# Attention and two expert layers: values read without the rows that chunks share, gate parts side by side

## The chip, the cores and the metric

The kernel runs on one core of a Trainium2 chip. The metric is the device time of one execution in microseconds; several executions are timed and their median is given. The core has five engines with a queue of instructions each: TensorE (PE, with its weight loads as PEld), VectorE (DVE), ScalarE (ACT), GpSimd (POOL) and SyncE (SP, which here only issues DMA transfers). Instructions of one queue start in order; queues wait for each other through semaphores.

## The reference

Three layers follow each other: a chunked attention, a mixture of experts with two experts for each token, and one with a single expert. All is float32.

```python
def _attn_ref(q, k, v, mem_k, mem_v):          # 4 batches, 8 heads, 768 positions, 64 per head
    chunk, left_ctx, right_ctx = (32, 16, 8)
    for c in range(S // chunk):
        k_full = concat(mem_k, k[l_start:r_end])      # 8 memory rows + up to 56 context rows
        v_full = concat(mem_v, v[l_start:r_end])
        scores = scale * q_c @ k_full.T
        a = softmax(scores)                           # sum + 1e-9
        out[c_start:c_end] = a @ v_full

def _moe_ref(x, w_gate, w_noise, noise, w1, w2):      # 3072 tokens of 512, 8 experts of 1024
    noisy = x @ w_gate + log1p(exp(x @ w_noise)) * noise
    top2, top2_w = two largest, softmax over the two
    out[mask] += top2_w * (relu(x[mask] @ w1[e]) @ w2[e])

def _moe2_ref(x, w_gate, w1, w2):
    expert, gate_w = argmax and softmax probability of x @ w_gate
    out[mask] = gate_w * (relu(x[mask] @ w1[e]) @ w2[e])
```

A chunk's 64 rows of values are 16 rows left of it, its own 32, 8 right of it, and 8 of memory. Neighbouring chunks share rows: the last 24 of a chunk's 56 context rows are the first 24 of the next chunk's.

## The kernel before, in words

The 3072 tokens are 24 tiles (`NT`) of 128 tokens; a tile is four chunks of 32 positions of one batch, with all 8 heads. The attention runs as a pipeline over tiles, written out in `build` (lines 1237 to 1284): iteration `t` does `scores(t)`, `flip(t - 1)`, `exp(t)`, `values(t - 2)`, `turn(t - 3)` and `logits(t - 4)`, in this order on every engine. No scheduler moves anything: each engine's queue has the order of the code.

`load` (line 274) reads a tile's queries, keys and values on the SP queue into one of five buffers `x`: the keys `k` as one transfer of 128 partitions (L278), and the queries with the values as two of 64 partitions each (L283). The lower 64 partitions hold the heads of one half, the upper 64 those of the other; the values of both stand in columns of their own, with zeros opposite (`clear`, lines 264 and 265), so that one matmul serves two heads. A chunk's 64 value rows are the 64 partitions of a half, its columns 260 of the 1040 (`VN`): the host lays the rows out chunk by chunk, those that chunks share several times, with a column of ones behind each head for the sum.

`scores` (L296) multiplies queries by keys into PSUM, and DVE takes the maximum (L303) and subtracts it (L305). `exp` (L311) is one ACT instruction of 512 columns. `flip` (L318, L320) transposes the result. `values` (L334) multiplies by the values, issues `load(t + 5)` for the buffer that has come free, and divides: DVE reads the sums (L340, L341), scales (L343) and casts to float16 (L347); POOL subtracts to get the low half of the number (L348), and SP stores both halves (L354). `turn` (L361, L362) transposes them, and `logits` (L373) multiplies the tile by the router's weights.

Every product is made of three float16 products: a number is a high and a low part, and high x high, high x low and low x high are added. `logits` so does 12 pairs of a weight load and a matmul for each tile, three for each of four slices of 512, into 16 columns of PSUM:

```python
for k in range(4):
    for a, w in ((0, 0), (0, 1), (1, 0)):
        nc.tensor.matmul(self.LG[b][:, j, :], y[:, a, k, :], self.wrh[:, w, k, :], ...)
```

`route` (line 377) runs once for each batch of six tiles: it reads these logits from PSUM (L385, L390), chooses two experts for each token and builds the tables by which the expert layers gather.

In the first expert layer (`Moe1`), 17 groups of up to 416 tokens go through `mlp`: matmuls `ph` (L523), ReLU in two parts (L525, L526), matmuls `py` (L534). `finish` (line 630) scales a block of 128 tokens, scatters it, splits it (`rest`, line 653), transposes it, and multiplies it by the second layer's gate weights, again 12 pairs (L666), now into 8 columns. L669 scales these into SBUF, and they are scattered. `Router2` adds them, takes the maximum and, in `prob` (line 767), the exponential. The second expert layer (`Moe2`) follows. Meanwhile the weights come in by `stage` transfers on SP and are split by ACT (L123) and DVE (L124).

Of the kernel before, what the change touches and what calls it, by code (L numbers as in the profile page):

```python
# [6 lines left out]
F32 = mybir.dt.float32  # L7
# [11 lines left out]
TB = S // 128  # L19
# [5 lines left out]
QV = QN + VN  # L25
# [206 lines left out]

def parts(nc, pool, src, n, name):
# [10 lines left out]
class Attention:  # L244


    def __init__(self, tc, g, qkv, ld, wk):
        nc = self.nc = tc.nc
        c = g.c
        self.tc, self.g, self.qkv, self.ld, self.wk = tc, g, qkv, ld, wk  # L250
        self.EE, self.ET, self.XT, self.LG, self.W = {}, {}, {}, {}, {}
        self.X = [ld.tile([128, 2 * QV + KN], F32, name=f"x{u}") for u in range(LK)]
# [9 lines left out]
    def clear(self, u):  # L262
        x = self.X[u]
        self.nc.vector.memset(x[64:128, KN:KN + QV], 0.0)  # L264
        self.nc.gpsimd.memset(x[0:64, KN + QV:], 0.0)
# [8 lines left out]
    def load(self, t, what="kqv"):  # L274

        x, y = self.X[t % LK], self.qkv[t]
        if "k" in what:
            self.nc.sync.dma_start(x[:, 0:KN], y[:, 0:KN])  # L278
        n = QN * ("q" in what) + VN * ("v" in what)
        for u in range(2):  # L280
            p = slice(64 * u, 64 * u + 64)
            o = KN if u == ("q" in what) else KN + QV - n
            self.nc.sync.dma_start(x[p, u * QV + o:u * QV + o + n], y[p, o:o + n])  # L283

    def scores(self, t):
# [4 lines left out]
        k = x[:, 0:KN].rearrange("p (b k) -> p b k", b=4)  # L290
        q = x[:, KN + VN:KN + VN + 2 * QN].rearrange("p (q b c) -> p b c q", b=4, c=4)
# [30 lines left out]
    def values(self, t):  # L322
# [4 lines left out]
        for a in range(2):  # L327
            for u in range(2):
                for ch in range(4):
                    i = KN + (D + 1) * (4 * ch + 2 * a + u)  # L330
                    v = x[:, i:i + D + 1]
                    v = bass.AP(tensor=v.tensor, offset=v.offset, ap=[v.ap[0], [QV + QN, 2], v.ap[1]])
# [31 lines left out]
    def logits(self, t):  # L364
# [3 lines left out]
        if j == 0:  # L368
            self.LG[b] = self.g.psr.tile([128, TB, 16], F32, name="lg")
        n = 0  # L370
        for k in range(4):
            for a, w in ((0, 0), (0, 1), (1, 0)):
                nc.tensor.matmul(self.LG[b][:, j, :], y[:, a, k, :], self.wrh[:, w, k, :],  # L373
                                 start=(n == 0), stop=(n == 11))
                n += 1

    def route(self, b):
# [3 lines left out]
        l = self.LG.pop(b)  # L381
# [161 lines left out]
class Moe1:  # L543
# [86 lines left out]
    def finish(self, p, gate, idx, group=None, lg=None):  # L630
# [22 lines left out]
        def rest(lg):  # L653
# [7 lines left out]
            if lg is None:  # L661
                lg = g.psr.tile([128, TB, 16], F32, name="lg")[:, 0, 0:E]
# [836 lines left out]
```

## Time and profile before

| what | us |
|---|---|
| three timed runs, median | 1055.11 |
| lowest and highest | 1054.06, 1056.59 |
| the profiled execution, its time | 1055.31 |
| its span in the profile | 1053.5 |
| PE busy | 980.5 (93%) |
| DVE busy | 486.7 (46%) |
| POOL busy | 423.3 (40%) |
| ACT busy | 377.6 (36%) |

The span is the part of the execution from the first to the last recorded instruction; 1.8 us lie around it. Busy time of PE counts pipelined matmuls with modelled ends, so 93% doesn't mean that PE is at its peak. The attention lies in the first 150 us, the first expert layer from there to about 760 us, the second behind it. A mean over the whole span mixes these three, so the views that follow are taken by stretch.

### The profile page before, as it was taken

How to read it: one execution, taken by the hardware profiler on the slowest of the kernel's cores; microseconds unless marked ns; L12 is line 12 of the kernel's file. 1: busy time of each engine (PE TensorE's matmuls, PEld its weight loads, DVE VectorE, ACT ScalarE, POOL GpSimd, SP SyncE). 2: the span in 40 equal slices, each digit the busy share in tenths (PEclk: the TensorE clock that was granted, in tenths of full speed). 3: DMA queues.
4: the chain of work that ended last, by engine and by line, in shares of the span. 5: the costliest groups of instructions: out<-in, count | busy, mean ns of one | idle time of the engine just before them, and what ended most of it. 6: DMA issues, size and time to landing. Idle time of an engine off the chain costs nothing.

```text
span 1053.5 us, 19188 instructions
## 1 busy us (share of the span) xinstructions
PE 980.5 (93%) x7599; PEld 585.0 (56%) x7599; DVE 486.7 (46%) x1015; ACT 377.6 (36%) x601; POOL 423.3 (40%) x420
## 2 busy tenths in 40 slices
PE   4899878999989999999999999989988998999998
PEld 3788755656545555454555555554564564555665
DVE  7567686542413432242234223475564355555511
ACT  1344344222323333233333233344313354454421
POOL 2222232334534454634554445434317255343421
PEclk9999979999999999989999999999998999999999
DMA  9999959745746776766687568489337679988640
GB/s 219 272 281 301 279 142 276 173 91 122 173 102 166 156 178 150 165 134 147 161 180 151 136 150 173 104 247 270 82 121 201 180 189 248 275 169 257 143 63 18
DMA packets 190146, 185.55 MB, mean 176 GB/s; under 512 B 151414, under 2 KB 152310, under 8 KB 190048
## 3 DMA queue, kind: packets, MB, share of 16 engines
q1 hardware_dynamic: 167664, 136.03, 56.4%
q0 software_dynamic: 21952, 48.07, 15.0%
q8 instruction: 62, 1.02, 0.4%
q14 instruction: 36, 0.29, 0.1%
q10 hardware_dynamic: 432, 0.15, 0.1%
HBM read 123.07 MB, written 39.53 MB: 154 GB/s over the span
## 4 chain that ended last, share of the span: by engine, by line
PE 45%; issue 12%; POOL 5%; DMA 4%; DVE 3%; ACT 1%; POOLq 0%; DVEq 0%; ACTq 0%; SPq 0%
PE ph L523 22%; PE py L534 20%; PE pr L716 2%; DMA xt<-x 2%; POOL out_dram L1037 1%; POOL x L1018 1%; DMA stage<-in_v_dram 1%; POOL gs L990 1%; PE lg L666 1%; POOL xp L990 1%; DVE w L124 1%; ACT w L123 1%; DMA xp<-Y,tbr 1%; DVE hT L526 0%; DMA xT<-xg 0%
## 5 line engine op out<-in xcount | busy, mean ns | idle before, releaser
L523 PE MATMUL ph<-xT,w 128*128 128x384 f16 (+3 forms) x2688 | 427.2, 318 | 23.3 <-DVE hT L526 10.8
L534 PE MATMUL py<-w,hT 128*128 128x512 f16 x1800 | 394.0, 379 | 0.0
L523 PEld LDWEIGHTS <-w 128*128 128x128 f16 x2688 | 263.1, 99 | 170.3 <-issue 31.3
L534 PEld LDWEIGHTS <-hT 128*128 128x128 f16 x1800 | 175.7, 98 | 207.3 <-issue 0.3
L526 DVE SCALAR_TENSOR_TENSOR hT<-ph,hT 128x384 f16<-128x384 f32 (+3 forms) x224 | 115.6, 521 | 254.8 <-ACT hT L525 218.1
L124 DVE SCALAR_TENSOR_TENSOR w<-stage,w 128x1024 f16<-128x1024 f32 x128 | 169.1, 1325 | 67.4 <-ACT w L123 62.2
L525 ACT ACTIVATE hT<-ph 128x384 f16<-128x384 f32 (+3 forms) x224 | 102.8, 462 | 232.9 <-PE ph L523 203.4
L123 ACT ACTIVATE w<-stage 128x1024 f16<-128x1024 f32 x128 | 133.5, 1049 | 23.9 <-DMA stage<-in_v_dram 18.5
L634 ACT ACTIVATE y<-py,gs 128x512 f32<-128x512 f32 x48 | 33.0, 687 | 190.4 <-PE py L534 134.1
L637 POOL DMA_INDIRECT Y<-y,t3y x43 | 44.4, 1034 | 115.7 <-ACT y L634 102.2
L655 DVE SCALAR_TENSOR_TENSOR x<-y,x 128x512 f16<-128x512 f32 x50 | 34.5, 690 | 119.8 <-ACT x L651 72.7
L637 POOL DMA_INDIRECT L<-l,t3y x43 | 45.0, 1047 | 101.4 <-DVE l L669 99.0
L1037 POOL DMA_INDIRECT out_dram<-y,tbo x22 | 23.7, 1076 | 128.0 <-ACT y L1036 102.5
L348 POOL TENSOR_TENSOR x<-x,x 128x512 f16<-128x512 f32 x24 | 29.4, 1226 | 112.7 <-DVE x L347 100.3
L296 PE MATMUL s<-x 128*64 128x64 f32 x768 | 50.3, 288 | 22.9 <-DVE x L264 10.6
L591 POOL DMA_INDIRECT Y<-ol,late x48 | 55.4, 1155 | 16.4 <-issue 16.4
L296 PEld LDWEIGHTS s<-x 128*64 128x64 f32 x768 | 47.0, 209 | 24.9 <-issue 23.3
L1036 ACT ACTIVATE y<-py,gs 128x512 f32<-128x512 f32 x27 | 18.5, 685 | 86.1 <-PE py L534 53.8
L565 POOL DMA_INDIRECT xg<-X,t3x x43 | 42.2, 981 | 15.1 <-issue 14.6
L565 POOL DMA_INDIRECT gs<-G,t3g x41 | 38.8, 946 | 12.5 <-issue 12.5
L1018 POOL TENSOR_TENSOR x<-xp 128x512 f32<-128x512 f32 x27 | 36.0, 1354 | 16.2 <-DVE xg L1021 9.9
L334 PE MATMUL o<-x,et 128*32 128x130 f32 x768 | 31.6, 307 | 3.8 <-DVE x L343 3.1
(267 smaller groups left out, 634.9 us busy)
## 6 DMA issues: line engine op xcount, KB each, us to landing
stage<-in_w_dram SPq DMA_DIRECT2D x64, 512.0 KB
stage<-in_v_dram SPq DMA_DIRECT2D x64, 512.0 KB
x<-in_qkv_dram SPq DMA_DIRECT2D x46, 388.0 KB
x<-in_qkv_dram SPq DMA_DIRECT2D x24, 368.0 KB
X<-x SPq DMA_DIRECT2D x24, 256.0 KB
xT<-xg SPq DMA_TRANSPOSE x75
xt<-x SPq DMA_TRANSPOSE x52
Y<-ol,late POOLq DMA_INDIRECT x48
```

The costliest lines, as they stand in the source:

```text
L123: nc.scalar.activation(hi, src, AF.Copy, scale=SW)
L124: return lambda v=nc.vector: v.scalar_tensor_tensor(lo, src, SW, hi, op0=OP.mult, op1=OP.subtract)
L296: nc.tensor.matmul(s[o:o + 64, ch // 2, b], q[:, b, ch], k[:, b, 40 * ch:40 * ch + 64], start=True, stop=True)
L523: nc.tensor.matmul(p[:, :n], w1[:, a, k, f, :], xT[:, b, k, :n], start=(i == 0), stop=(i == 11))
L525: nc.scalar.activation(hT[:, 0, f, :n], p[:, :n], AF.Relu)
L526: nc.vector.scalar_tensor_tensor(hT[:, 1, f, :n], p[:, :n], 0.0, hT[:, 0, f, :n], op0=OP.max, op1=OP.subtract)
L534: nc.tensor.matmul(p[:m], hT[:, a, f, o:o + m], w2[:, c, f, :], start=(i == 0), stop=(i == 23))
L565: self.nc.gpsimd.indirect_dma_start(out=out, out_offset=None, in_=src, in_offset=IO(ap=idx, axis=0))
L591: st = nc.gpsimd.indirect_dma_start(out=self.Y, out_offset=IO(ap=idx[:, i:i + 1], axis=0), in_=z, in_offset=None, bounds_check=2 * N - 1, ...
L637: st = nc.gpsimd.indirect_dma_start(out=dst, out_offset=IO(ap=idx, axis=0), in_=src, in_offset=None, bounds_check=2 * N - 1, oob_is_err=False)
L655: nc.vector.scalar_tensor_tensor(w[:, DM:], y, SX2, w[:, :DM], op0=OP.mult, op1=OP.subtract)
L1018: nc.gpsimd.tensor_tensor(s, x[:, :DM], x[:, DM:], op=OP.add)
```

## The change

Four things change.

1. **Loads.** Queries and keys come as one tensor `qk`, values as two: `va` has the 32 rows of each chunk that no other chunk starts with, once, and `vb` the last 24 rows of the tile's fourth chunk and the 8 memory rows, once. `load` issues seven transfers for three: 64 partitions of keys and lower queries (L289), 64 of keys (L290), 64 of upper queries (L291), and for each half 32 of `va` (L295) and 32 of `vb` (L296).
2. **Copies on the chip.** `spread` is new and stands behind `scores(t)` in each iteration. For each half, POOL copies `vb`'s 260 columns to the three other chunks (L303, 32 partitions), and then writes over 24 of these partitions with the next chunk's rows, which stand in the first 24 partitions one chunk further (L305).
3. **Order of the 64 rows.** Since the 24 shared rows now stand ahead of the 8 memory rows, `exp` writes its 64 columns in three pieces (32, 24 and 8) in the new order.
4. **Gates.** `gating` replaces both loops of 12: the high and the low weights stand side by side, so that the high part of the tokens is loaded once and multiplied by both, into 2n columns, and the low part goes onto the second n. `route` adds the two halves with two more DVE instructions; in the second layer L669 becomes a reduction, and its scale moves into the exponential in `prob`.

```diff
-QV = QN + VN
+QK = QN + KN
+VC = VN // 4
+XK, XQ, XU, XV = VN, VN + KN, VN + QK, VN + QK + QN
...
+def gating(nc, out, xT, w, n):
+    for k in range(4):
+        nc.tensor.matmul(out[:, 0:2 * n], xT[:, 0, k, :], w[:, :, k, :], start=(k == 0), stop=False)
+        nc.tensor.matmul(out[:, n:2 * n], xT[:, 1, k, :], w[:, 0, k, :], start=False, stop=(k == 3))
...
     def clear(self, u):
         x = self.X[u]
-        self.nc.vector.memset(x[64:128, KN:KN + QV], 0.0)
-        self.nc.gpsimd.memset(x[0:64, KN + QV:], 0.0)
+        self.nc.vector.memset(x[64:128, 0:VN], 0.0)
+        self.nc.vector.memset(x[64:128, XQ:XU], 0.0)
+        self.nc.gpsimd.memset(x[0:64, XU:], 0.0)
...
-    def load(self, t, what="kqv"):
-        x, y = self.X[t % LK], self.qkv[t]
-        if "k" in what:
-            self.nc.sync.dma_start(x[:, 0:KN], y[:, 0:KN])
-        n = QN * ("q" in what) + VN * ("v" in what)
+    def load(self, t, what="qv"):
+        x, dma = self.X[t % LK], self.nc.sync.dma_start
+        if "q" in what:
+            dma(x[0:64, XK:XU], self.qk[t, 0:64])
+            dma(x[64:128, XK:XQ], self.qk[t, 64:128, 0:KN])
+            dma(x[64:128, XU:XV], self.qk[t, 64:128, KN:])
+        if "v" in what:
+            for u in range(2):
+                p, o = 64 * u, XV * u
+                dma(x[p:p + 32, o:o + VN], self.va[t, 32 * u:32 * u + 32])
+                dma(x[p + 32:p + 64, o + 3 * VC:o + VN], self.vb[t, 32 * u:32 * u + 32])
+
+    def spread(self, t):
+        x = self.X[t % LK]
         for u in range(2):
-            p = slice(64 * u, 64 * u + 64)
-            o = KN if u == ("q" in what) else KN + QV - n
-            self.nc.sync.dma_start(x[p, u * QV + o:u * QV + o + n], y[p, o:o + n])
+            p, o = 64 * u, XV * u
+            self.nc.gpsimd.tensor_copy(x[p + 32:p + 64, o:o + 3 * VC].rearrange("p (c v) -> p c v", c=3),
+                                       x[p + 32:p + 64, None, o + 3 * VC:o + VN].to_broadcast([32, 3, VC]))
+            self.nc.gpsimd.tensor_copy(x[p + 32:p + 56, o:o + 3 * VC], x[p:p + 24, o + VC:o + VN])
...
     def exp(self, t):
-        self.nc.scalar.activation(e, d, AF.Exp, scale=0.125)
+        for i, o, n in ((0, 0, 32), (32, 40, 24), (56, 32, 8)):
+            self.nc.scalar.activation(e[:, :, :, i:i + n], d[:, :, :, o:o + n], AF.Exp, scale=0.125)
...
     def logits(self, t):
-        n = 0
-        for k in range(4):
-            for a, w in ((0, 0), (0, 1), (1, 0)):
-                nc.tensor.matmul(self.LG[b][:, j, :], y[:, a, k, :], self.wrh[:, w, k, :],
-                                 start=(n == 0), stop=(n == 11))
-                n += 1
+        gating(nc, self.LG[b][:, j], y, self.wrh, 16)
...
     def route(self, b):
-        l = self.LG.pop(b)
+        lg = self.LG.pop(b)
+        l = rr.tile([128, TB, 16], F32, name="l16")
+        V.tensor_copy(l, lg[:, :, 16:])
+        V.tensor_tensor(l, l, lg[:, :, :16], op=OP.add)
...
-            i = 0
-            for k in range(4):
-                for a, c in ((0, 0), (0, 1), (1, 0)):
-                    nc.tensor.matmul(lg, t[:, a, k, :], g.wg2[:, c, k, :], start=(i == 0), stop=(i == 11))
-                    i += 1
+            gating(nc, lg, t, g.wg2, E)
             l = g.mo.tile([128, E], F32, name="l", bufs=4)
-            nc.vector.tensor_scalar(l, lg, 1.0 / (SX2 * SG), None, op0=OP.mult)
+            with nc.allow_low_precision("float32"):
+                nc.vector.tensor_reduce(l, lg[:, 0:2 * E].rearrange("p (a e) -> p e a", a=2), axis=AX.X, op=OP.add)
...
-            nc.scalar.activation(l, l, AF.Exp)
+            nc.scalar.activation(l, l, AF.Exp, scale=1.0 / (SX2 * SG))
...
                 if t < NT:
                     at.scores(t)
+                    at.spread(t)
```

The first place is the SP queue in the steady attention, one tile with its store and the transfer that follows. `X_62` is the stored array, `x_88` and so on are the five buffers, and in brackets stands what an instruction waits for; DMAHW0 to DMAHW7 are the semaphores of earlier transfers, which new transfers take in turn. Before:

```order
L278 DMA x_88<-in_qkv_dram 128x736 [waits DMAHW2_49]
L283 DMA x_88<-in_qkv_dram 64x1552 [waits DMAHW3_49,PE_49]
L283 DMA x_88<-in_qkv_dram 64x1552 [waits DMAHW4_49]
L354 DMA X_62<-x_701 128x1024 [waits DMAHW5_49,Pool_49]
L278 DMA x_89<-in_qkv_dram 128x736 [waits DMAHW6_49]
```

And with the change:

```order
L289 DMA x_88<-in_qk_dram 64x1248 [waits DMAHW0_49]
L290 DMA x_88<-in_qk_dram 64x736 [waits DMAHW1_49]
L291 DMA x_88<-in_qk_dram 64x512 [waits DMAHW2_49]
L295 DMA x_88<-in_va_dram 32x1040 [waits DMAHW3_49,PE_49]
L296 DMA x_88<-in_vb_dram 32x260 [waits DMAHW4_49]
L295 DMA x_88<-in_va_dram 32x1040 [waits DMAHW5_49]
L296 DMA x_88<-in_vb_dram 32x260 [waits DMAHW6_49]
L378 DMA X_62<-x_784 128x1024 [waits DMAHW7_49,Pool_49]
L289 DMA x_89<-in_qk_dram 64x1248 [waits DMAHW0_49]
```

Four transfers of a tile have become eight. Each waits for the one eight places ahead: that was the same transfer two tiles back and is now the same transfer of the tile before. The store still waits for POOL.

The second place is the POOL queue at the same time. Before, it holds one subtraction for each tile:

```order
L348 TENSOR_TENSOR x_536<-x,x_536 128x512 [waits DVE_49,DMAHW5_49,PE_49,Pool_49]
L348 TENSOR_TENSOR x_619<-x,x_619 128x512 [waits DVE_49,DMAHW1_49,PE_49,Pool_49]
L348 TENSOR_TENSOR x_701<-x,x_701 128x512 [waits DVE_49,DMAHW5_49,PE_49,Pool_49]
L348 TENSOR_TENSOR x_783<-x,x_783 128x512 [waits DVE_49,DMAHW1_49,PE_49,Pool_49]
L348 TENSOR_TENSOR x_865<-x,x_865 128x512 [waits DVE_49,DMAHW5_49,PE_49,Pool_49]
```

With the change, four copies stand between one subtraction and the next:

```order
L372 TENSOR_TENSOR x_696<-x,x_696 128x512 [waits DVE_49,DMAHW7_49,PE_49,Pool_49]
L303 COPY x_90<-x_90 32x780 [waits DMAHW4_49,Pool_49]
L305 COPY x_90<-x_90 24x780 [waits DMAHW3_49,Pool_49]
L303 COPY x_90<-x_90 32x780 [waits DMAHW6_49]
L305 COPY x_90<-x_90 24x780 [waits DMAHW5_49,Pool_49]
L372 TENSOR_TENSOR x_784<-x,x_784 128x512 [waits DVE_49,DMAHW7_49,PE_49,Pool_49]
```

The copies of tile `t` (here in `x_90`) wait for that tile's four value transfers, and the subtraction of tile `t - 2` stands behind them.

## Rows read from the trace of the kernel before

**Rows 1.** Busy time by stretch: us, engines' busy time (x count), PE clock, DMA share, GB/s

```profile
20.00:40.00 20.00, 17.90 (x308) 15.07 (x307) 12.87 (x27) 6.88 (x11) 4.81 (x4) 0.91 1.03 262
30.00:85.00 55.00, 50.77 (x923) 44.64 (x923) 35.30 (x107) 24.02 (x35) 11.64 (x10) 0.94 1.03 278
120.00:140.00 20.00, 17.56 (x340) 15.78 (x340) 13.37 (x56) 8.41 (x14) 5.98 (x6) 1.00 0.77 223
300.00:400.00 100.00, 96.86 (x625) 51.34 (x624) 33.40 (x53) 33.72 (x54) 43.80 (x42) 0.98 0.66 149
```

**Rows 2.** Transfers of 30 to 85 us: issues of one kind, count, KB each

```profile
x<-in_qkv_dram SPq DMA_DIRECT2D x22, 388.0 KB
x<-in_qkv_dram SPq DMA_DIRECT2D x11, 368.0 KB
X<-x SPq DMA_DIRECT2D x10, 256.0 KB
```

**Rows 3.** The SP queue's waits of 0 to 140 us: total, times, longest

```profile
SPq L354 <- POOL x L348: 31.2, 15, 6.1
SPq L283 <- DMA x<-in_qkv_dram: 13.6, 16, 1.4
```

**Rows 4.** PE in order of time in the attention: start, us, line, operation

```profile
91.07 1.09 PE L334 MATMUL o<-x,et 128*32 128x130 f32 x32
...
92.55 0.45 PE L373 MATMUL lg<-wr,xt 128*128 128x16 f16 x12
...
92.93 2.08 PE L296 MATMUL s<-x 128*64 128x64 f32 x32
...
95.52 1.42 PE L334 MATMUL o<-x,et 128*32 128x130 f32 x32
```

**Rows 5.** Busy time by stretch at the start, columns as in the first group

```profile
9.20:11.20 2.00, 0.63 (x12) 0.66 (x13) 1.73 (x2) 0.00 (x0) 0.00 (x0) 1.00 0.99 214
13.20:14.40 1.20, 0.00 (x0) 0.00 (x0) 1.05 (x2) 0.09 (x1) 0.00 (x0) 1.00 1.20 303
14.50:16.40 1.90, 1.90 (x32) 1.88 (x32) 1.35 (x1) 0.45 (x1) 0.00 (x0) 1.00 1.04 225
```

**Rows 6.** The tile x from 0 to 90 us: shortest, median and longest issue, ns

```profile
L283 SPq DMA_DIRECT2D x<-in_qkv_dram x38: 465/472/1320, 1.2 to 89.5; - x38
```

**Rows 7.** Groups by line of 0 to 140 us: busy us, mean ns, idle before

```profile
L348 POOL TENSOR_TENSOR x<-x,x 128x512 f16<-128x512 f32 x21 | 24.4, 1163 | 104.4 <-DVE x L347 95.2 <-DVE s L301 4.8 <-PE s L296 4.4
...
L343 DVE TENSOR_TENSOR x<-o,r 128x512 f32<-128x512 f32 x21 | 14.5, 692 | 2.4 <-DVE r L341 0.5
...
L311 ACT ACTIVATE e<-d 128x512 f32<-128x512 f32 x23 | 14.5, 629 | 20.3 <-DVE d L305 18.5 <-DVE r L340 1.5 <-issue 0.3
...
L265 POOL MEMSET x<- 64x1552 f32 x5 | 6.8, 1453 | 0.0
...
L347 DVE CAST x<-x 128x512 f16<-128x512 f32 x21 | 9.0, 427 | 4.0 <-DMA X<-x 3.5
...
L385 ACT ACTIVATE ex<-lg 128x48 f32<-128x48 f32 x3 | 0.6, 205 | 0.0
```

**Rows 8.** PE in order of time in the first expert layer

```profile
221.35 0.45 PE L666 MATMUL lg<-wg,xt 128*128 128x8 f16 x12
221.66 4.06 PE L523 MATMUL ph<-xT,w 128*128 128x384 f16 x24
```

**Rows 9.** The tile lg: shortest, median and longest, ns; first and last start

```profile
L669 DVE TENSOR_SCALAR l<-lg x50: 151/159/168, 208.4 to 756.5; 128x8 f32<-128x8 f32 x50
```

**Rows 10.** The chain that ended last, shares by line

```profile
by line: PE ph L523 21.7%; PE py L534 19.9%; issue 11.8%; PE pr L716 2.1%; DMA xt<-x 1.5%; POOL out_dram L1037 1.4%; POOL x L1018 1.3%; DMA stage<-in_v_dram 1.3%; POOL gs L990 1.1%; PE lg L666 1.1%; POOL xp L990 1.1%; DVE w L124 0.7%; ACT w
```

**Rows 11.** All engines in order of time at the start

```profile
1.13 0.26 DVE L186 CAST diag<-diag_i 128x128 f32<-128x128 int32 x1
...
1.98 6.17 DVE L186 CAST iota<-iota_i 128x144 f16<-128x144 int32 x1
...
2.60 5.46 POOL L265 MEMSET x<- 64x1552 f32 x4
```

More of the change, by code (lines that the diff above doesn't have):

```diff
@@ L244, with __init__ @@
 class Attention:
-    def __init__(self, tc, g, qkv, ld, wk):
+    def __init__(self, tc, g, qk, va, vb, ld, wk):
         nc = self.nc = tc.nc
         c = g.c
-        self.tc, self.g, self.qkv, self.ld, self.wk = tc, g, qkv, ld, wk
+        self.tc, self.g, self.qk, self.va, self.vb, self.ld, self.wk = tc, g, qk, va, vb, ld, wk
         self.EE, self.ET, self.XT, self.LG, self.W = {}, {}, {}, {}, {}
-        self.X = [ld.tile([128, 2 * QV + KN], F32, name=f"x{u}") for u in range(LK)]
+        self.X = [ld.tile([128, XV + VN], F32, name=f"x{u}") for u in range(LK)]
         self.stores = []
@@ L368, in logits @@
         if j == 0:
-            self.LG[b] = self.g.psr.tile([128, TB, 16], F32, name="lg")
-        n = 0
-        for k in range(4):
-            for a, w in ((0, 0), (0, 1), (1, 0)):
-                nc.tensor.matmul(self.LG[b][:, j, :], y[:, a, k, :], self.wrh[:, w, k, :],
-                                 start=(n == 0), stop=(n == 11))
-                n += 1
+            self.LG[b] = self.g.psr.tile([128, TB, 32], F32, name="lg")
+        gating(nc, self.LG[b][:, j], y, self.wrh, 16)
     def route(self, b):
@@ L661, in rest @@
             if lg is None:
-                lg = g.psr.tile([128, TB, 16], F32, name="lg")[:, 0, 0:E]
-            i = 0
-            for k in range(4):
-                for a, c in ((0, 0), (0, 1), (1, 0)):
-                    nc.tensor.matmul(lg, t[:, a, k, :], g.wg2[:, c, k, :], start=(i == 0), stop=(i == 11))
-                    i += 1
+                lg = g.psr.tile([128, TB, 32], F32, name="lg")[:, 0]
+            gating(nc, lg, t, g.wg2, E)
             l = g.mo.tile([128, E], F32, name="l", bufs=4)
-            nc.vector.tensor_scalar(l, lg, 1.0 / (SX2 * SG), None, op0=OP.mult)
+            with nc.allow_low_precision("float32"):
+                nc.vector.tensor_reduce(l, lg[:, 0:2 * E].rearrange("p (a e) -> p e a", a=2), axis=AX.X, op=OP.add)
             scatter(self.L, l)
@@ L1123, in over1 @@
             nc.sync.dma_start_transpose(out=xT.rearrange("p a k q -> p (a k) q"), in_=xg)
-            for _ in mlp(tc, g, key, [128], xT, lambda b, m, p: m1.finish(p, gs, idx[2], lg=pp[:, 400:408])):
+            for _ in mlp(tc, g, key, [128], xT, lambda b, m, p: m1.finish(p, gs, idx[2], lg=pp[:, 400:416])):
                 pass
@@ L1195, in over2, with build @@
                 pass
-def build(tc, qkv, noise, wr, wg2, w1, w2, v1, v2, out):
+def build(tc, qk, va, vb, noise, wr, wg2, w1, w2, v1, v2, out):
     nc = tc.nc
@@ L1225, in build @@
             ld = ctx.enter_context(tc.tile_pool(name="ld", bufs=1))
-            at = Attention(tc, g, qkv, ld, wk)
+            at = Attention(tc, g, qk, va, vb, ld, wk)
             at.ps = ctx.enter_context(tc.tile_pool(name="psa", bufs=1, space=PSUM))
-            at.load(0, "kq")
+            at.load(0, "q")
             at.load(0, "v")
@@ L1448, in layouts, with values @@
     p = pad(inp["v"])
-    w = np.stack([np.concatenate([p[:, :, 32 * c:32 * c + 32], inp["mem_v"], p[:, :, 32 * c + 32:32 * c + 56]], axis=2)
-                  for c in range(S // 32)], axis=2)
-    w = split(w, (TB, 4, 64, D)).transpose(0, 4, 3, 6, 5, 1, 2, 7)
-    v = np.ones(w.shape[:-1] + (D + 1,), f)
-    v[..., :D] = w
-    v = v.reshape(NT, 128, VN)
-    lower, upper = slice(0, 64), slice(64, 128)
-    qkv = np.concatenate([np.concatenate([k[:, lower], v[:, lower], q[:, lower]], axis=2),
-                          np.concatenate([k[:, upper], q[:, upper], v[:, upper]], axis=2)], axis=1)
+    def values(w, c):
+        w = split(w, (TB, c, 32, D)).transpose(0, 4, 3, 6, 5, 1, 2, 7)
+        v = np.ones(w.shape[:-1] + (D + 1,), f)
+        v[..., :D] = w
+        return v.reshape(NT, 64, c * VC)
+    va = values(p[:, :, :S], 4)
+    vb = values(np.concatenate([x for j in range(TB) for x in (p[:, :, 128 * j + 128:128 * j + 152], inp["mem_v"])],
+                               axis=2), 1)
+    qk = np.concatenate([k, q], axis=2)
     def rows(w):
@@ L1466, in layouts @@
     return {
-        "qkv": qkv,
+        "qk": qk, "va": va, "vb": vb,
         "noise": inp["moe_noise"].reshape(NT, 128, E).transpose(1, 0, 2).reshape(128, NT * E),
```

8 lines of the change are left out of this document (4 added, 4 removed).

## The prediction, made before the change was run

> **What bounds the kernel now.** I read four views in this order: the busy table by stretch, the transfers and the SP queue's waits of the attention, PE in order of time, and the groups by line.
>
> The table [rows 1] splits the run. From 20 to 40 us, as in the whole stretch from 30 to 85, the sixteen DMA engines are at their limit (share 1.03), while PE is busy 18 of 20 us: the attention is paced by its transfers, with PE close behind. From 300 to 400 us PE is busy 96.9 of 100 us and DMA two thirds: the first expert layer is paced by PE. What is saved in loads counts in the first stretch, what is saved in matmuls in the second.
>
> From 30 to 85 us the transfers run at 278 GB/s [rows 1]. One tile is a load of 368 KB, two of 388 KB and a store of 256 KB [rows 2], 1400 KB or 1.434 MB: 5.16 us a tile. The SP queue waits most for the subtraction L348 ahead of the store and then for older transfers [rows 3]. PE does one tile at full clock in the 4.45 us from one block of values (91.07) to the next (95.52), of which the logits take 0.38 (92.55 to 92.93) [rows 4]. Over the stretch PE is busy 50.77 of 55 us [rows 1], 4.76 us a tile with the router's matmuls. So if the loads shrink, PE lets 0.4 to 0.5 us a tile through.
>
> **The loads.** A tile's loads go from 1144 KB (1.171 MB) to 312 + 184 + 128 + 2 x (130 + 32.5) = 949 KB (0.972 MB), 17% fewer bytes. But the 368 KB load covered all 128 partitions; now every load covers 64 or 32. Two stretches of the start in which little but a 64-partition load is under way run at 214 and 225 GB/s, one that is mostly the 128-partition load at 303 [rows 5]. With 220 and 303: before 377 kB / 303 + 795 kB / 220 = 1.24 + 3.61 = 4.85 us, and the 0.31 us missing to 5.16 is what the store adds. After: 972 kB / 220 + 0.31 = 4.73 us, a gain of 0.43 us a tile. Lower end: all halves at 214, 4.85 us, gain 0.31. Upper end: the stretch's own 278 GB/s holds for smaller pieces too, which swap halves more often and may overlap: 1.234 MB / 278 = 4.44 us, gain 0.72. It applies to some 20 tiles; the last ones (120 to 140 us, DMA share 0.77 [rows 1]) are paced by something else. PE stands at about 4.7, and two limits so close don't interlock perfectly, so I book the lower end, 0.3 us a tile: **-6.0 us** (up to 24 x 0.72 = 17.3 were the loads alone the bound).
>
> **The SP queue** issues eight transfers a tile for four. An issue of this kind has a median of 0.47 us [rows 6]: the four added ones cost 1.9 us of SP a tile and all eight 3.8, below 4.7. As the order rows show, a transfer waits for the one eight places ahead of it, so one tile is in flight where there were two. Its 4.4 us of queued data cover an issue; I cost it at nothing. If they don't, one bare issue a tile, 0.47 x 20 = 9 us, eats the gain.
>
> **POOL** gets four copies a tile, each 780 elements long. No row shows a POOL copy. Below: the memset L265, 1453 ns for 1552 elements, 0.94 ns each, so 0.73 us. Above: the subtraction L348, which reads two streams, 1163 ns for 512, 2.27 ns each, so 1.77 us [rows 7]. I take 0.75 us: a copy has one stream in and one out, nearer to the memset. Four copies and L348 make 4 x 0.75 + 1.16 = 4.16 us a tile, under 4.73. They stand in the queue ahead of the subtraction of the tile two back, for which the store on SP and the turn on PE one iteration later wait. A tile's values (333 kB at 220, 1.5 us) land behind its keys, so the copies end some 4.5 us after the keys. The cast L347 that the subtraction needs comes after scores and flip (92.93 to 95.52), values (1 us) and L343 with two short DVE instructions (1 us) [rows 4, 7]: 4.6 us after the keys. The cover holds, barely. I cost POOL at nothing.
>
> The Trainium skill (GPSIMD Engine Reference, Engine selection) says that one-input work on this engine runs at roughly line rate; no row here shows it.
>
> **The exponent** in three pieces: L311 takes 629 ns for 512 columns and L385 205 for 48, so 0.91 ns a column and 0.16 us fixed: 3 x 0.16 + 512 x 0.00091 = 0.95 us, 0.32 more [rows 7]. ACT is busy 24 of 55 us [rows 1], and the flip that reads the result comes an iteration later: hidden, 24 x 0.32 = 7.7 us if not. The memsets keep their size.
>
> **The gates.** Each gating goes from 12 load-and-multiply pairs to 8. In the expert layer 12 pairs move the next matmul by 0.31 us (221.35 to 221.66) [rows 8]; there are 50 such blocks [rows 9], a third less is 50 x 0.10 = 5.2 us. The chain that ended last holds 1.1% of 1053.5 us, 11.6 us, in that line [rows 10]; a third is 3.9 us. Between them **-4.5 us**, nearly all in the stretch that PE paces. The attention's 24 blocks (24 x 0.13 = 3.0 us) hide behind the loads. DVE's read L669 becomes a reduction to the same 8 columns, off the path. The router reads its logits through a copy and an addition, each a little over L669's 159 ns [rows 9], four times; DVE's wait for the logits costs nothing, since its next reduction waits for scores that stand behind them on PE. The last router stands on the path: **+0.5 us**. The scale that moves into the exponential costs nothing.
>
> **Sum.** The profiled execution took 1055.31 us, 0.2 us above the median of the runs shown: 1055.3 - 6.0 - 4.5 + 0.5 = **1045.3 us**.
>
> **Rivals.**
> (a) POOL becomes the bound, slower. A DVE cast took 0.26 us, the next 6.17 us while POOL's memsets ran, and it ended when they did [rows 11]: a DVE instruction can stand still for a whole row of POOL's. If L347 (0.43 us [rows 7]) and POOL exclude each other, POOL's turn of a tile is 4c + 1.16 + 0.43, with c for a copy. It passes 5.16 at c = 0.89, and from c = 0.97 it costs more than the gates' net 4.0 and 2.1 us beyond. In the middle of the bounds, c = 1.25: 6.59 us, (6.59 - 5.16) x 20 = 28.6, so 1055.3 + 28.6 - 4.0 = 1080; at c = 1.77 it is 1121. Against it: the memset's price, and that the cast comes when the copies are mostly over. The Trainium skill (SBUF — State Buffer, two separate sides) calls the port pair that these two engines share an exclusive lock, held for a whole instruction; the 6.17 us agree. Chance 0.20.
> (b) The loads gain nothing: every piece runs at the rate of the half loads and the smaller ones lose the rest at their ends. Only the gates count: 1055.3 - 4.0 = 1051.3. For it speak 214 and 225 against 303 GB/s [rows 5]; against it, that even at 214 throughout the bytes give 0.31 us a tile. The Trainium skill (SBUF — State Buffer, The DMA port swizzle) says that 64 partitions reach half of the memory's ports, and 32 no fewer; by that rule, splitting the 368 KB load undoes most of what the missing rows save. The rows agree on the halves. Chance 0.22.
> (c) The rate holds with the bytes: 17.3 us, 1055.3 - 17.3 - 4.0 = 1034; with PE's limit of 0.5 us on 20 tiles 1041; I put it at 1037. Chance 0.13.
> (d) The gates don't do what they say: 12 x 8 columns before, 4 x 16 + 4 x 8 now, the same 96. Were a pair's price its columns, the 4.5 us are gone: 1049.8. Against it: in the attention 12 pairs of 16 columns cost 0.38 us, not twice the 0.31 of 8 columns [rows 4, 8]. Chance 0.05.
>
> **How the numbers follow.** The forecast has the remaining 0.40. A measurement of this kernel can tell about 0.2%, 2.1 us, from no change. Faster: the forecast but for 0.03 of it, (c), (d) and 0.17 of (b): 0.72. Same: 0.05 of (b) and that 0.03: 0.08. Slower: (a), 0.20. The range goes from just under (c), 1036, over (d) and (b) into the foot of (a) (c = 1.02, 1062), which leaves out under 2 in 10.
>
> **What would show it.** Right: the copies L303 and L305 near 0.75 us; tiles every 4.8 to 4.9 us between 30 and 85 us; the gating blocks of the expert layer moving the next matmul by 0.2 us; PE's first expert matmul some 6 us earlier. Wrong: copies over 0.95 us, or POOL busy from end to end of the attention (a); the DMA share still at its limit with fewer GB/s (b); gaps in the DMA share while SP issues (one tile in flight).

## The result, and the profile after

The changed kernel took **1043.17 us** (median of 8 runs, 1035.05 to 1047.39) against 1055.18 for the kernel before on the same chip (8 runs, 1052.65 to 1065.08): ratio 0.9861, 95% interval 0.9827 to 0.9895, so 11 to 18 us less by the interval. 1045.3 was forecast. The profiled execution is the fastest of the eight, 1035.05 us, so the two profiles differ by 20 us where the medians differ by 12.

The same stretches as in [rows 1], columns as there (the cores' engines, then PE's granted clock, DMA share and GB/s):

```profile
20.00:40.00 20.00, 18.05 (x311) 15.20 (x310) 14.06 (x29) 8.78 (x21) 18.46 (x20) 0.91 0.94 238
30.00:85.00 55.00, 48.54 (x847) 41.84 (x843) 40.68 (x107) 23.47 (x51) 46.83 (x51) 0.95 0.95 247
120.00:140.00 20.00, 12.01 (x221) 10.09 (x220) 16.74 (x61) 7.02 (x18) 13.48 (x16) 0.86 0.57 150
300.00:400.00 100.00, 98.07 (x606) 51.40 (x605) 33.89 (x54) 34.03 (x54) 46.56 (x45) 1.00 0.63 154
```

Two things changed in the steady attention. The DMA engines are no longer full, and they move less in the same time (247 GB/s for 278). And POOL, the fifth engine of the row, went from 11.6 to 46.8 us of 55. From 120 to 140 us PE does only 12.0 us of work instead of 17.6. The groups of 0 to 140 us that answer to [rows 7]:

```profile
L305 POOL COPY x<-x 24x780 f32<-24x780 f32 x45 | 40.2, 893 | 2.8
L303 POOL COPY x<-x 32x780 f32<-32x780 f32 x45 | 39.0, 867 | 7.5 <-DMA xg<-X,t1x 3.0 <-DMA x<-in_vb_dram 1.9
L372 POOL TENSOR_TENSOR x<-x,x 128x512 f16<-128x512 f32 x20 | 23.2, 1160 | 16.0 <-DVE x L371 4.1 <-PE misc L467 3.9 <-DMA x<-in_va_dram 2.5
...
L371 DVE CAST x<-x 128x512 f16<-128x512 f32 x21 | 11.8, 561 | 8.5 <-DMA X<-x 7.9
```

A copy takes 0.88 us. The subtraction is as long as before, and the cast ahead of it takes 561 ns instead of 427.

The stores leave at 32.76 us (tile 1) and 78.04 (tile 10), so tiles follow each other every 5.03 us; before it was 32.40 and 81.46, 5.45 us. But the last values of the attention start later, before:

```profile
148.23 1.96 PE L334 MATMUL o<-x,et 128*32 128x130 f32 x32 [2.12 <-DVE x L343]
```

and after:

```profile
152.41 2.04 PE L358 MATMUL o<-x,et 128*32 128x130 f32 x32 [2.56 <-ACT w L125]
```

So in these two executions what the attention had won is gone at its end. Two of PE's waits of 85 to 150 us have grown, one for POOL and one for DVE (total, times, longest; some of such a wait can be made up later, so they don't add up to a loss). Before:

```profile
PE misc L223 <- DVE two L408: 1.7, 1, 1.7
...
PE xp L361 <- POOL x L348: 0.3, 1, 0.3
```

And with the change:

```profile
PE xp L385 <- POOL x L372: 7.2, 4, 5.8
PE misc L225 <- DVE two L430: 4.4, 1, 4.4
```

The longest wait for POOL, 5.8 us, stands behind one subtraction, that of the 20th tile. Here POOL also issues the transfers that gather rows for the first experts (L587; start, us, line):

```profile
129.84 0.43 DVE L371 CAST x<-x 128x512 f16<-128x512 f32 x1
...
130.34 0.96 POOL L587 DMA_INDIRECT xg<-X,t1x  x1 [0.30 <-issue]
...
134.26 0.83 POOL L303 COPY x<-x 32x780 f32<-32x780 f32 x1 [2.95 <-DMA xg<-X,t1x]
...
137.87 1.15 POOL L372 TENSOR_TENSOR x<-x,x 128x512 f16<-128x512 f32 x1
...
139.08 0.61 PE L385 MATMUL xp<-ident,x 128*128 128x128 f16 x4 [5.78 <-POOL x L372]
```

The cast that the subtraction needs ended at 130.27. But four copies stand ahead of the subtraction in POOL's queue, and the first of them started, by the profile, only when the gather had landed. So the subtraction began 7.6 us after its cast. Before, it followed within 0.3 us, behind the same gather:

```profile
129.92 0.96 POOL L565 DMA_INDIRECT xg<-X,t1x  x1 [0.30 <-issue]
...
132.99 0.43 DVE L347 CAST x<-x 128x512 f16<-128x512 f32 x1
...
133.66 1.16 POOL L348 TENSOR_TENSOR x<-x,x 128x512 f16<-128x512 f32 x1 [2.78 <-DVE x L347]
```

At the wait for `two` it is DVE that is late (DVE in order of time):

```profile
101.03 0.71 DVE L424 CAST eid<-i 128x12 f32<-128x12 uint32 x1
101.77 0.26 DVE L427 TENSOR_TENSOR oh<-iota,eid 128x96 f16<-128x96 f16 x1
102.06 0.69 DVE L430 TENSOR_TENSOR two<-oh 128x48 f16<-128x48 f16 x1
```

and POOL in the same stretch:

```profile
100.88 0.83 POOL L303 COPY x<-x 32x780 f32<-32x780 f32 x1
101.76 0.96 POOL L305 COPY x<-x 24x780 f32<-24x780 f32 x1
```

`eid` has 12 columns and takes 0.71 us: it ends as the first copy ends. `two` has 48 and ends with the second. Before, they were short:

```profile
102.09 0.16 DVE L402 CAST eid<-i 128x12 f32<-128x12 uint32 x1
...
102.58 0.18 DVE L408 TENSOR_TENSOR two<-oh 128x48 f16<-128x48 f16 x1
```

In between `oh`, which started with the second copy, kept its usual 0.26, and that copy took 0.96 instead of 0.83.

The gating in the first expert layer, which answers to [rows 8] (eight rows for a block now):

```profile
221.93 0.17 PE L238 MATMUL lg<-wg,xt 128*128 128x16 f16 x1
...
222.11 0.17 PE L239 MATMUL lg<-wg,xt 128*128 128x8 f16 x1
222.14 4.06 PE L545 MATMUL ph<-xT,w 128*128 128x384 f16 x24
```

A block moves the next matmul by 0.21 us, where it was 0.31.

### The profile page after: what moved, and what is told of

The parts are those of the page before. It is cut to its first block, busy times and chain, and to the rows that moved or that the text cites. A ratio compares the mean times of both kernels' runs of the same rounds, so it can differ in the third digit from the quotient of the medians.

```text
span 1033.3 us, 18951 instructions
## 1 busy us (share of the span) xinstructions
PE 963.3 (93%) x7303; PEld 573.2 (55%) x7303; DVE 505.0 (49%) x1028; ACT 382.3 (37%) x649; POOL 510.2 (49%) x516
## 4 chain that ended last, share of the span: by engine, by line
PE 40%; issue 14%; POOL 6%; DMA 4%; DVE 4%; ACT 1%; another core or an unknown queue 0%; POOLq 0%; DVEq 0%
PE py L556 19%; PE ph L545 19%; POOL x L1037 2%; DMA xp<-Y,ter 2%; POOL out_dram L1056 1%; PE pr L735 1%; POOL gs L1009 1%; POOL xp L1009 1%; DMA stage<-in_v_dram 1%; DVE w L126 1%; ACT w L125 1%; DVE hT L548 1%; DMA xp<-Y,tbr 1%; DMA xt<-x 1%; PE lg L238 0%
## 5 line engine op out<-in xcount | busy, mean ns | idle before, releaser
L545 PE MATMUL ph<-xT,w 128*128 128x384 f16 (+3 forms) x2688 | 421.3, 315 | 19.5 <-DVE hT L548 9.1
L613 POOL DMA_INDIRECT Y<-ol,late x48 | 58.0, 1208 | 16.4 <-issue 16.4
L318 PE MATMUL s<-x 128*64 128x64 f32 x768 | 49.8, 291 | 12.2 <-DVE x L274 7.9
L318 PEld LDWEIGHTS s<-x 128*64 128x64 f32 x768 | 46.3, 209 | 13.7 <-issue 9.7
L587 POOL DMA_INDIRECT xg<-X,t3x x43 | 42.1, 980 | 15.1 <-issue 14.6
L303 POOL COPY x<-x 32x780 f32<-32x780 f32 x48 | 41.6, 866 | 7.7 <-DMA xg<-X,t1x 3.0
L587 POOL DMA_INDIRECT gs<-G,t3g x41 | 38.8, 946 | 12.5 <-issue 12.5
L305 POOL COPY x<-x 24x780 f32<-24x780 f32 x48 | 42.7, 890 | 2.9
```

Of the source, the lines that this page charges most:

```text
L305: self.nc.gpsimd.tensor_copy(x[p + 32:p + 56, o:o + 3 * VC], x[p:p + 24, o + VC:o + VN])
L318: nc.tensor.matmul(s[o:o + 64, ch // 2, b], q[:, b, ch], k[:, b, 40 * ch:40 * ch + 64], start=True, stop=True)
L545: nc.tensor.matmul(p[:, :n], w1[:, a, k, f, :], xT[:, b, k, :n], start=(i == 0), stop=(i == 11))
L587: self.nc.gpsimd.indirect_dma_start(out=out, out_offset=None, in_=src, in_offset=IO(ap=idx, axis=0))
L613: st = nc.gpsimd.indirect_dma_start(out=self.Y, out_offset=IO(ap=idx[:, i:i + 1], axis=0), in_=z, in_offset=None, bounds_check=2 * N - 1, ...
```

## The experiments

The runs were made in three groups, each on one chip with runs of the kernel before beside them (medians 1058.64, 1046.92 and 1058.65 us). In the order in which the quoted texts count them, the first to fourth are gates alone, loads alone, copies of five tiles and half of the copies on ACT; the fifth to eighth issues on ACT, whole keys, sixteen pairs and five transfers; the ninth to twelfth gates in the expert layer, five transfers with all copies on POOL, five transfers with whole keys, and the change again. Times don't compare across groups. Ratios do if all kernels move with the kernel before, and why that one moved by 12 us between groups is not known.

**1. Which half of the change pays.** The hunks of the diff for `gating`, `logits`, `route`, `finish` and `prob` alone, put into the kernel before:

> The kernel before with the gates of the change alone (8 pairs for 12, the router's two more DVE instructions, the reduction and the moved scale); loads, copies and exponent as before. Theory A, the terms of the prediction: the gates are worth 4.0 us net, so 1051 against 1055 before, ratio 0.996. Theory B, from the trace of the changed kernel: since the attention there ends no earlier than before (last values at 152.4 us against 148.2), the gates and what hangs on them in the expert layers carry the whole gain of 12 us, so about 1043, ratio 0.988. By both, the attention's blocks of values stay where they were (within 1 us), and a gating block in the expert layer moves the next matmul by 0.20 us instead of 0.31.

And the changed kernel with the loops of 12 put back:

> The changed kernel with the old gates (12 pairs): loads, copies and the exponent in three pieces alone. Theory A: 6 to 8 us under the kernel before, 1047 to 1049, ratio 0.993. Theory B: what the loads win by 85 us is lost by 150 us, so 1053 to 1056, ratio 0.998 to 1.001.

Measured: gates alone 1048.14 us, ratio 0.9885 (0.9845 to 0.9926); loads alone 1056.66 us, 1.0003 (0.9974 to 1.0032). The loads, the copies and the exponent in pieces together gain nothing that can be told, and the gates make the whole difference. Theory B held for the times, theory A fell. What both expected of the attention failed: with the gates alone its last values came at 154.5 us, 6.3 later than before, where 1 us was allowed. The DMA engines were as full as before and moved 270 GB/s instead of 278, so the 148.2 us of before is one execution and no fixed mark (see the last section).

**2. What the copies cost.** The copies of the first five tiles alone (`LK` is 5):

```diff
-                    at.spread(t)
+                    if t < LK:
+                        at.spread(t)
```

> The changed kernel with the copies of the first five tiles only; later tiles use whatever rows stand in those partitions, so the shared rows of their values are not this tile's. Theory B says that the copies on POOL hold up DVE (small instructions of the router take 0.6 to 0.8 us instead of 0.2) and with it the end of the attention: without them the last values come at 140 to 144 us instead of 152.4, and the time falls by 8 to 12 us from the 1043 of the changed kernel, to 1031 to 1035. Its rival, that the rate of the partial loads paces the tiles and POOL is only beside them: same places within 2 us and 1041 to 1045.

The last values came at 142.85 us, 9.6 us earlier than with all copies. Its whole time (1132 us) can't be compared, since other values send the tokens to other experts. The router's rows on DVE of 85 to 150 us (busy us, mean ns), with the change:

```profile
L436 DVE TENSOR_TENSOR vr<-eid,vr 128x12 f32<-128x12 f32 x2 | 1.5, 766 | 0.0
L430 DVE TENSOR_TENSOR two<-oh 128x48 f16<-128x48 f16 x2 | 1.5, 736 | 0.1
```

and without the later copies:

```profile
L430 DVE TENSOR_TENSOR two<-oh 128x48 f16<-128x48 f16 x2 | 0.4, 183 | 0.1
L436 DVE TENSOR_TENSOR vr<-eid,vr 128x12 f32<-128x12 f32 x2 | 0.3, 172 | 0.0
```

So the copies hold DVE up: it is busy 31.3 of the 35 us from 85 to 120 with them, 25.1 without. And the 20th subtraction follows its cast in 0.24 us again. The starts of POOL's subtractions show where the 9.6 us arise. With and without the later copies, the 9th starts at 64.2 and 64.1 us, the 12th at 83.4 and 80.3, the 19th at 127.5 and 120.2, the 21st at 142.8 and 133.4. Most of it, 7.3 us, is lost by the 19th, while DVE is the fuller for the copies, and some 2 us more between the 19th and the 21st, where the copies stand behind the gather. All ten profiled executions with copies in the late tiles have that gap ahead of the 20th subtraction (5.7 to 8.1 us), and the four without have 0.24. But tiles did not come faster early on: 5.11 us each from tile 1 to 10. What paces them there is something else.

**3. Half of the copies on ACT.**

```diff
+            copy = self.nc.scalar.copy if u else self.nc.gpsimd.tensor_copy
-            self.nc.gpsimd.tensor_copy(...)
+            copy(...)
```

> The changed kernel with the two copies of the upper half on ACT instead of POOL. ACT then has about 2.5 + 2 x 0.87 = 4.2 us of work in a tile, POOL 2 x 0.88 + 1.16 = 2.9 instead of 4.7. Theory B: half of what the copies cost comes back, 4 to 6 us, so 1037 to 1039. The rival, that ACT's own work (exponent, flip, turn) comes late behind copies that wait for DMA: 1043 to 1050, with PE waiting for et or xp of ACT.

1039.75 us, 0.9844 (0.9803 to 0.9886), too near the change's 0.9861 to tell apart by the time; the last values say more: 147.1 us, 5.3 earlier than the change's profile, about half of the 9.6, as theory B had it.

**4. What paces the tiles.** Issues of L291 and L296 moved from SP to ACT (`other` is SP's queue for the first five tiles, then ACT's):

```diff
-            dma(x[64:128, XU:XV], self.qk[t, 64:128, KN:])
+            other(x[64:128, XU:XV], self.qk[t, 64:128, KN:])
...
+                other(x[p + 32:p + 64, o + 3 * VC:o + VN], self.vb[...])
```

> The changed kernel with three of a tile's seven load transfers (the upper queries and both vb) issued by ACT instead of SP; bytes, pieces and copies stay. Between 30 and 85 us the changed kernel moves 247 GB/s with its queue at 93.7%, and SP waits only 7 us of 55: eight issues of 0.4 to 0.6 us a tile fill it. Theory C, that SP's issues and the one tile in flight open the gaps: queue share over 99%, 260 GB/s or more, a tile 0.3 us sooner, last values 3 to 6 us earlier where the router's delays leave it, time 1038 to 1041 on the scale of 1055 before. Rival D, that partial transfers are slower in themselves: share up to 100%, but GB/s stay within 245 to 252 and the time within 2 us of the changed kernel's ratio of 0.986.

Moving the issues made it worse: 1.0027 (1.0000 to 1.0055), 219 GB/s, last values at 168.4 us. SP's own issues then last 27.9 us of 55, but it waits 24.7 us for older transfers and POOL, 11.9 of them for upper queries that ACT now issues. Of the two longest rows the first is of this kind, the second waits for SP's own transfers:

```profile
SPq L296 <- DMA x<-in_qk_dram: 9.3, 2, 5.8
SPq L290 <- DMA x<-in_qk_dram: 5.8, 5, 2.4
```

That run decides nothing between the theories. Then the keys as one transfer:

```diff
+            dma(x[:, XK:XQ], self.qk[t, :, 0:KN])
+            dma(x[0:64, XQ:XU], self.qk[t, 0:64, KN:])
+            dma(x[64:128, XU:XV], self.qk[t, 64:128, KN:])
```

> The changed kernel with the keys as one transfer of 128 partitions and the queries as two of 64 (seven load transfers a tile, as in the change, and the same bytes). Rival D: the rate of 30 to 85 us rises from 247 to 255 GB/s or more at the same share of the queue, time 2 to 4 us less, 1039 to 1041. Theory C: as many issues and as many gaps, 244 to 250 GB/s, time within 2 us of the change, ratio 0.984 to 0.988.

Time and rate stayed (0.9868, 0.9832 to 0.9904; 247 GB/s), as theory C had it, but the DMA engines became idler, which neither theory had said. The hardware queue of 30 to 85 us (packets, MB, share of the 16 engines), in the change and with whole keys:

```profile
q1 hardware_dynamic: 6274, 13.45, 93.7%
```

```profile
q1 hardware_dynamic: 6965, 13.45, 84.3%
```

The same 13.45 MB need a tenth less of the engines when the keys go to 128 partitions, and the tiles come no faster for it: 4.93 us each. The Trainium skill (SBUF — State Buffer, The DMA port swizzle) says that 64 partitions reach half the ports; the two shares agree that halves cost engine time. They also show that engine time was not the limit here.

**5. Fewer transfers.** Values next to queries in memory, so that five transfers carry a tile's loads:

```diff
+            dma(x[64:128, XK:XQ], ku)
+            dma(x[0:32, 0:XU], la)
+            dma(x[32:64, 3 * VC:XU], lb)
+            dma(x[64:96, XU:], ua)
+            dma(x[96:128, XU:XV + VC], ub)
```

> The kernel of the fourth run (upper copies on ACT) with a tile's loads in five transfers instead of seven: own rows with keys and queries of the lower half in one of 32 partitions, the shared rows with theirs in another, the keys of the upper half, and the same two for the upper half, whose chunks stand in reversed order so that vb lies next to the queries. Same bytes. Theory C: SP issues six transfers a tile, about 3 us; queue share over 99% between 30 and 85 us, last values 3 to 5 us earlier than in the fourth run (147.1 us), time 1035 to 1037, ratio 0.981 to 0.983. Rival D: transfers of 32 partitions are no better, 240 to 250 GB/s, ratio 0.984 as in the fourth run, or worse where a load of 300 KB now waits for the values of the tile that leaves the buffer.

1022.14 us, **0.9775** (0.9740 to 0.9809). Queue share 98.4%, 265 GB/s, a tile every 4.78 us, last values at 141.0 us, 6.1 earlier than with seven transfers: more than theory C had promised, as is the ratio (0.9775 for 0.981 to 0.983), with a share a little under its 99%. The same with `copy = self.nc.gpsimd.tensor_copy` for both halves:

> The eighth run's five transfers with all four copies on POOL, as in the change: against the change only the number and the cut of the transfers differ. Theory C: 260 GB/s or more between 30 and 85 us and a tile every 4.7 to 4.8 us there; POOL then has 4 x 0.88 + 1.16 = 4.7 us of it, so it is at its limit too; the router's delays stay, last values at 146 to 149 us, ratio 0.980 to 0.983. Its rival, that the eighth run owes its gain to having half the copies on ACT: 0.985 to 0.988, last values at 151 us and later.

1041.24 us, 0.9828 (0.9784 to 0.9872), but the last values at 152.6 us as in the change: at that place the rival was right, and theory C's 260 GB/s and 4.7 to 4.8 us a tile did not come (243 and 5.20). The first tiles ran at 263 GB/s (20 to 40 us); from 60 to 85 only 207. POOL was as busy there as in the change (19.5 of 25 us), but now SP waited for the subtraction there, ahead of the store, 13.5 us of the 55 from 30 to 85, where in the change it had waited 1.4:

```profile
SPq L389 <- POOL x L383: 13.5, 8, 4.1
```

Fewer transfers help when POOL has room, and not before. And with whole keys besides, ahead of the lower values in the buffer:

```diff
-            dma(x[64:128, XK:XQ], ku)
+            dma(x[:, 0:KN], k)
```

> The eighth run (upper copies on ACT) with the keys again as one transfer of 128 partitions: keys, then for each half own rows with queries and shared rows with queries, five in all, and the same bytes. In the sixth run whole keys took the queue's share from 93.7% to 84.3% at the same 247 GB/s, 293 GB/s at a full queue; so here the transfers alone would need 1.234 MB / 293 = 4.2 us a tile and PE sets the pace with 4.6 to 4.7. Expected: queue share 90 to 95% at 262 to 270 GB/s, last values at 138 to 141 us, ratio 0.974 to 0.978. Rival: PE, DVE and ACT already set the pace in the eighth run, nothing changes, 0.9775.

1027.46 us, **0.9693** (0.9649 to 0.9736): the lowest ratio of all, under the range that was expected, and 20 us below the change in the same group. Queue share 94.8%, 263 GB/s, last values at 139.5 us, 1.5 earlier than with five transfers alone. That whole keys add anything to five transfers is not shown by the time: the two ran in different groups, and the time itself is 5 us longer here than there. The change itself in the same group:

> The changed kernel itself once more, on the chip of these runs: ratio 0.983 to 0.990 as before, last values at 151 to 154 us, 240 to 250 GB/s between 30 and 85 us. What its profile says of PE's clock and of the blocks near 304 and 445 us tells how far the first profile (20 us under that of before, where the medians differ by 12) was a lucky one: if the medians are right, more of its execution is at half clock than there.

1047.29 us, 0.9885 (0.9842 to 0.9927), last values at 154.0 us, 249 GB/s.

The attention of all these kernels in one table. "SP" is the sum of the durations of SP's issues that start from 30 to 85 us, transfers include the store:

| kernel | transfers a tile | copies | queue share, GB/s | SP, us | last values, us | ratio |
|---|---|---|---|---|---|---|
| before | 4 | none | 101.7%, 278 | 21.6 | 148.2 | 1 |
| gates alone | 4 | none | 101.8%, 270 | 18.0 | 154.5 | 0.9885 |
| change | 8 | POOL | 93.7%, 247 | 43.9 | 152.4 | 0.9861 |
| change, again | 8 | POOL | 95.7%, 249 | 46.3 | 154.0 | 0.9885 |
| loads alone | 8 | POOL | 95.2%, 244 | 46.1 | 154.2 | 1.0003 |
| first five copied | 8 | POOL, five tiles | 94.0%, 245 | 47.3 | 142.9 | - |
| half on ACT | 8 | both | 92.7%, 241 | 46.7 | 147.1 | 0.9844 |
| whole keys | 8 | POOL | 84.3%, 247 | 44.7 | 152.3 | 0.9868 |
| five loads | 6 | both | 98.4%, 265 | 31.6 | 141.0 | 0.9775 |
| five loads, POOL | 6 | POOL | 90.1%, 243 | 30.8 | 152.6 | 0.9828 |
| five loads, whole keys | 6 | both | 94.8%, 263 | 31.8 | 139.5 | 0.9693 |

With eight transfers SP issues for 44 to 47 of 55 us, waits only 2 to 7, and the rate stays at 241 to 249 GB/s, whatever the copies or the keys do. With six it issues for 31 to 32 and waits 19 to 21: it is no longer the limit, and where POOL isn't full, 263 to 265 GB/s are moved. Six transfers for eight also let more of a tile be in flight at once. No run separates that from the issues, but with eight SP waits for older transfers 0.8 to 4.7 of 55 us, so the single tile in flight can cost little beside them.

**6. The price of the gates.** Each block of the expert layer twice:

```diff
             gating(nc, lg, t, g.wg2, E)
+            gating(nc, lg[:, 2 * E:], t, g.wg2, E)
```

> The changed kernel with each gating of the expert layer done twice, the second time into columns that nobody reads: 16 pairs for 8 in 50 blocks. By the direct price of a pair (0.0255 us, from 0.204 us for a block of 8) this costs 8 x 0.0255 x 50 = 10 us: 1053, and nothing else changes. Theory E, that blocks of many short instructions also leave PE without instructions behind them where a block stands between the matmuls pr (there the block of before lasts 3.6 and 3.8 us instead of 0.3, and PE runs at half clock after it): 15 to 20 us more than the change, 1058 to 1063, and the blocks near 304, 445 and 590 us last 3.5 us and more.

Sixteen pairs: 1047.45 us, 0.9996 (0.9973 to 1.0019), 0.0128 x 1047 = 13 us more than the whole keys with 8 pairs on the same chip, a little over the direct 10. A block lasts 0.41 us, as the direct price says, and the blocks at the three places are short (0.71, 0.48, 0.49 us): theory E fell in this form. Nor does the time follow the number of pairs alone: 16 pairs cost no more than the 12 old ones of the loads alone (1.0003, in another group), though a block takes 0.41 us with 16 and 0.31 with 12. And the hunks for `gating`, `finish` and `prob` alone, without `logits` and `route`:

> The kernel before with the 8 pairs in the expert layer alone; the router of the attention keeps its 12 pairs and its reads. By the direct price, 50 blocks x 0.10 = 5 us: 0.995. By theory E (some of the time is that PE waits for instructions around three blocks near 304, 445 and 590 us, and runs at half clock behind them) 8 to 12 us: 0.989 to 0.992, with those three blocks together shorter than the 8.4 us of before. The rival that the router's part carries the difference to the 11 us of the first run: 0.995 and the three blocks as before.

1039.70 us, 0.9792 (0.9739 to 0.9844), more than either theory had, and more than the gates with the router's part (0.9885, in another group). So the direct price of 5 us is seen in every trace, and the time moves by more.

Two more terms can be read from PE's rows, in one execution of each kernel: before and loads alone with 12 pairs; gates alone, gates in the expert layer and the change twice with 8. From the start of a block to PE's next other matmul, the blocks of a run sum to 23.2 and 22.4 us with 12 pairs and to 16.4, 13.3, 12.6 and 15.5 with 8, so 7 to 11 us less and not 5. The surplus lies in the three blocks ahead of `pr` matmuls that the expectation names: 8.4 and 7.6 us together with 12 pairs, 6.2, 3.2, 2.5 and 5.4 with 8 (and 1.7 with 16). And the matmuls `ph` and `pr`, the same in number everywhere, are busy 455.2 and 450.9 us with 12 pairs and 448.7, 444.6, 444.5 and 453.4 with 8. The last two are one kernel, so a single execution doesn't tell how much of this the gates cause.

The first profile of the change and the second differ most plainly at the first `pr` matmuls, with the same instructions. First profile:

```profile
301.31 2.77 PE L735 MATMUL pr<-w,rh 128*32 128x512 f16 x24
...
305.94 2.77 PE L735 MATMUL pr<-w,rh 128*32 128x512 f16 x24 [1.58 <-PEq L1079]
```

Second profile:

```profile
303.37 2.77 PE L735 MATMUL pr<-w,rh 128*32 128x512 f16 x24
...
309.57 5.31 PE L735 MATMUL pr<-w,rh 128*32 128x512 f16 x24 [3.15 <-PEq L1079]
```

PE waits there for its own sequencer, 1.58 us or 3.15, and after the longer wait the 24 matmuls take 5.31 us instead of 2.77: the lower of the clock's two levels, 1.2 instead of 2.4 GHz (the granted clock is 0.50 from 309.57 to 314.88 us, and 1.00 in the 2.77 us at 303.37). From the first expert matmul to the end of the last one the two executions of one kernel took 872.0 and 884.5 us. Single executions with 12 pairs took 897 (before) and 888 (loads alone), those with 8 took 868 to 887, and the one with 16 took 883 (the run with copies of five tiles, which sends tokens elsewhere, left out). **What stays open:** why the gates' 5 us become 8 to 16, or 16 to 28 in the expert layer alone. Waits of this kind and the clock behind them are where the traces differ, but no run set them on purpose.

## Why the prediction was right, point by point

The number was right (1045.3 forecast, 1043.17 measured, inside the range), and that was luck: of -6.0 us booked for the loads nothing came, and of -4.0 net for the gates -12.2 did. The two errors, 6.3 and 8.2 us, cancel but for 2.

- **Loads, -6.0 us: failed.** Alone they measured +0.3 us (-2.8 to +3.4). A tile's gain came out inside what was derived, 0.42 us (5.45 to 5.03) for 0.31 to 0.72, but not for its reason: the DMA rate fell from 278 to 247 GB/s and SP set the pace. The old loads, too, took 5.68 and 5.76 us a tile in two other executions (gates alone, gates in the expert layer). What failed is the step "I cost POOL at nothing": the copies cost 9.6 us by the end of the attention, which took the gain back.
- **POOL.** c was 0.88 us, between 0.75 and the 0.97 from which rival (a) wins. 4 x 0.88 + 1.16 = 4.7 us a tile is under the 5.03 that a tile takes, so the turn of a tile never became the bound as (a) priced it. Its mechanism was there all the same, at a place that I hadn't named: the router's many short DVE instructions, each of which can wait out a copy (`two`: 0.74 us for 0.18), and PE behind them. I had looked for the lock only at the cast. "The cover holds, barely" failed as well, at one tile: behind the gather the 20th subtraction started 7.6 us after its cast; elsewhere in that trace it was 2.6 at most. I had not counted the gathers in POOL's queue. The Trainium skill (SBUF — State Buffer, two separate sides) calls the shared ports an exclusive lock; `eid` and `two` ending with the copies agree.
- **SP, "I cost it at nothing": failed.** I reckoned 3.8 us of issues a tile, and they take 43.9 x 5.03 / 55 = 4.0 us: nearly right. What failed is that the transfers in flight would cover them. With 7 of the 55 us of waits and some 4 between issues SP is never ahead. That is why a tile takes 5.03 and not the 4.8 to 4.9 that I named, and why 128-partition keys don't help while five transfers do. The sign that I had named, gaps in the DMA share while SP issues, is the one that appeared (0.95 for 1.03).
- **Rates of halves.** Right as a cost of the engines (84.3% against 93.7%), wrong as the limit.
- **The gates, -4.5 and +0.5 us: too small.** The blocks went from 0.31 to 0.21 us, fifty of them, as booked: 5 us. Alone the gates measured -12.2 (-8 to -16). Rival (d) is out. How the surplus comes about stays open. The router's two more instructions took 0.25 us each where a little over 0.16 was booked.
- **Exponent in pieces: right.** The three take 0.82 us together where 0.95 was derived, and ACT was 23.5 of 55 us busy, no more than before.
- **"PE's first expert matmul some 6 us earlier": wrong.** 155.8 us against 151.5.

Of the rivals, (b) came nearest in its outcome for the loads, not in its reason.

## What to carry to other kernels

Moving work to an engine that looks idle costs what it does to its neighbours: a copy of 0.88 us on POOL turned DVE instructions of 0.18 us into 0.74, and most of the price fell where DVE works in many short steps. A smaller part fell where the copies, waiting for something else in POOL's queue, kept back an instruction that was ready behind them. Bytes saved by cutting a load into more transfers are saved only if the issuing queue keeps up: sum its issues for one period and leave a margin, since 44 us of issues in 55 was already the limit. And a total that comes out right says little of its terms: the two halves of this change, run by themselves, came to 0.9885 and 1.0003 where 0.996 and 0.994 were booked.

## What the runs showed that I had not expected

- The DMA rate at a full queue differed between executions of the same loads: 278, 270 and 256 GB/s (before, gates alone, gates in the expert layer), and the attention with the old loads ended at 148.2, 154.5 and 156.7 us. Against the last two the change (152.4 and 154.0) is not later at all; what of the old attention's gain or loss is typical, three single executions don't tell. The kernels with eight transfers, all from SP, and all copies on POOL ended alike (152.3 to 154.2).
- One kernel's expert layers took 872.0 or 884.5 us, by waits of PE for its sequencer and its lower clock after them.
- The first scores started at 7.9 us instead of 10.6. POOL's memsets keep their size, as I had said, but the first copies now stand between them, so two run in a row and not four (2.80 us for 5.46), and the cast that stands still with them [rows 11] took 3.51 us instead of 6.17.
- Half of the copies on ACT (0.84 us each) end the attention 5.3 us earlier, five transfers alone not at all (152.6 us), and both together 11 us earlier (152.4 to 141.0).
